# A fused Hyena filter and gated MLP on one core: every other chunk's fraction made by ScalarE and VectorE instead of VectorE and GpSimd

## The chip, the core and the metric

One Trainium2 (trn2) chip, one of its cores. The metric is the device time of one execution in microseconds (us), measured on the chip. The kernel before takes 4258.93 us (median of three runs, 4258.6 to 4264.06; with a fourth run, 4258.99). Engines are named as the profile names them: PE is the matmul engine (PEld its weight loads), DVE is VectorE, ACT is ScalarE, POOL is GpSimd. In the traces each engine starts its instructions in the order of its own queue, and waits there for what another engine has to finish first (an example below: an ACT instruction whose input was ready started 0.71 us later, behind the one in front of it).

## The reference

Shortened:

```python
def _attn_ref(x, v, pos_emb, w1, w2):              # x, v: (4, 12480, 128)
    h_filt = (np.maximum(pos_emb @ w1, 0.0) @ w2) * np.exp(-0.01 * pos)[:, None]
    u = x * v
    y = irfft(rfft(u, 2*S) * rfft(h_filt, 2*S), 2*S)[:, :S, :]      # along the sequence
    return x * y

def _moe_ref(x, w_in, w_out):                      # x: (49920, 128), d_ff = 2048
    h = x @ w_in
    return (h * np.cos(h)) @ w_out
```

A long convolution for each of four batches, then an MLP whose activation is h cos(h). The change touches only the cosine.

## The kernel before

The convolution of a batch is a hand-made two-level Fourier transform, in five stages: u (multiply and fold the inputs; DVE and POOL), f1 (first transform; PE, evicted by ACT and DVE), f2 (second transform and the product with the filter; PE, four DVE products, two POOL sums), i1 and i2 (the inverse). Batch 0 is done first, alone. Then the MLP's *chunks* run, and the convolutions of batches 1 to 3 are woven in between them, one *unit* of convolution work for every 1.2 to 2.3 chunks, by stage (set in the kernel). When they are done, the MLP runs alone to the end. A chunk is 128 of the 2048 hidden columns for a *tile* of 480 tokens: 16 chunks a tile, 104 tiles, 1664 chunks.

cos(h) is made as sin(2 pi f), f being h/(2 pi) + 1/4 minus its nearest integer. So a chunk passes through PE, ACT, DVE, POOL, ACT, DVE and PE again (shortened, `...` and the tiles of cs and gt left out):

```python
def moe_up(pool, n, c):
    ph = ps_h.tile([P, BANK], F32, name="ph")                       # one of 4 PSUM banks
    nc.tensor.matmul(ph[:, 0:TOK], w_in_sb[:, c * P:(c + 1) * P], ats[n][:, :], ...)
    a = pool.tile([P, TOK], F32, name="a", bufs=3)
    nc.scalar.activation(a[:, :], ph[:, 0:TOK], AF.Identity,        # a = h/(2 pi) + 1/4
                         bias=quarter[:, 0:1], scale=INV_TWO_PI)
    k = pool.tile([P, TOK], F32, name="k")
    nc.vector.tensor_scalar(out=k[:, :], in0=a[:, :], scalar1=ROUND,   # k = round(a)
                            scalar2=ROUND, op0=ALU.add, op1=ALU.subtract)
    f = pool.tile([P, TOK], F32, name="f")
    nc.gpsimd.tensor_tensor(f[:, :], a[:, :], k[:, :], op=ALU.subtract)  # f = a - k
    return ph, f

def moe_act(pool, ph, f):
    nc.scalar.activation(cs[:, :], f[:, :], AF.Sin, scale=TWO_PI)
    nc.vector.tensor_tensor(gt[:, :], ph[:, 0:TOK], cs[:, :], op=ALU.mult)
    ...
# main loop, one step a chunk (cut):
for i in range(len(steps) + LAG):
    hidden[i] = moe_up(mpool, n, c)
    gates[i - 1] = moe_act(mpool, *hidden.pop(i - 1))     # one chunk behind
    moe_down(pn, pc, gates.pop(i - LAG))                  # four chunks behind
    ...                                                   # store, next tile's transposes
    while owed > 0.0:
        owed -= next(conv, owed)                          # units of convolution
```

Of the kernel before, what the change touches and what calls it, by code (L numbers as in the profile page):

```python
# [9 lines left out]
F32 = mybir.dt.float32  # L10
U32 = mybir.dt.uint32
AF = mybir.ActivationFunctionType
ALU = mybir.AluOpType
# [3 lines left out]
P = 128  # L17
# [5 lines left out]
TWO_PI = 6.283185  # L23

ROUND = 12582912.0
# [5 lines left out]
def kernel(  # L31
# [38 lines left out]
    nc = tc.nc  # L70
# [38 lines left out]
    cs = const.tile([N2, 3, H], F32, name="cs")  # L109
# [448 lines left out]
    def moe_turn(pool, n):  # L558
        zb = zbs.pop(n)
        pt = ps_h.tile([P, BANK], F32, name="ph")  # L560
        for m in range(TOK // N2):
            transpose(pt[:, m * N2:(m + 1) * N2], zb[:, m, :])
        at = pool.tile([D, TOK], F32, name="at")
        nc.vector.tensor_copy(out=at[:, :], in_=pt[:, 0:TOK])
        ats[n] = at

    def moe_up(pool, n, c):
        ph = ps_h.tile([P, BANK], F32, name="ph")
        nc.tensor.matmul(ph[:, 0:TOK], w_in_sb[:, c * P:(c + 1) * P], ats[n][:, :],  # L569
                         start=True, stop=True)  # L570
        a = pool.tile([P, TOK], F32, name="a", bufs=3)
        nc.scalar.activation(a[:, :], ph[:, 0:TOK], AF.Identity,  # L572
                             bias=quarter[:, 0:1], scale=INV_TWO_PI)
        k = pool.tile([P, TOK], F32, name="k")
        nc.vector.tensor_scalar(out=k[:, :], in0=a[:, :], scalar1=ROUND,  # L575
                                scalar2=ROUND, op0=ALU.add, op1=ALU.subtract)
        f = pool.tile([P, TOK], F32, name="f")
        nc.gpsimd.tensor_tensor(f[:, :], a[:, :], k[:, :], op=ALU.subtract)  # L578
        return ph, f

    def moe_act(pool, ph, f):
        cs = pool.tile([P, TOK], F32, name="cs")
        nc.scalar.activation(cs[:, :], f[:, :], AF.Sin, scale=TWO_PI)  # L583
        gt = pool.tile([P, TOK], F32, name="gt", bufs=4)
        nc.vector.tensor_tensor(gt[:, :], ph[:, 0:TOK], cs[:, :], op=ALU.mult)  # L585
        return gt

    def moe_down(n, c, gt):
        if c == 0:
            accs[n] = ps_acc.tile([P, BANK], F32, name="acc")  # L590
        nc.tensor.matmul(accs[n][:, 0:TOK], w_out_sb[:, c, :], gt[:, :],  # L591
                         start=(c == 0), stop=(c == NFC - 1))

    def moe_evict(pool, n):
        ot = pool.tile([D, TOK], F32, name="ot", bufs=1)
        nc.scalar.copy(out=ot[:, :], in_=accs.pop(n)[:, 0:TOK])
        return ot

    def moe_store(pool, n, ot):
        pt = ps_h.tile([P, BANK], F32, name="ph")  # L600
        for m in range(TOK // N2):
            transpose(pt[0:N2, m * D:(m + 1) * D], ot[:, m * N2:(m + 1) * N2])
        ob = pool.tile([N2, TOK // N2, D], F32, name="ob", bufs=1)
        nc.vector.tensor_copy(out=ob[:, :, :].rearrange("i m d -> i (m d)"),
                              in_=pt[0:N2, :])
        nc.sync.dma_start(
            out[n * TOK:(n + 1) * TOK, :].rearrange("(m p) d -> p m d", p=N2),
            ob[:, :, :])

    with tc.manual_schedule():  # L610
        make_identity(nc, ident)
        with tc.tile_pool(name="psum", bufs=8, space=PSUM) as psum, \
# [67 lines left out]
            wpool = ctx.enter_context(tc.tile_pool(name="weights", bufs=1))  # L680
            w_in_sb = wpool.tile([D, DFF], F32, name="w_in_sb")
            w_out_sb = wpool.tile([P, NFC, D], F32, name="w_out_sb")
            quarter = wpool.tile([P, 1], F32, name="quarter")
            nc.vector.memset(quarter[:, :], 0.25)
            nc.sync.dma_start(w_in_sb[:, :], wind[:, :])
            nc.sync.dma_start(w_out_sb[:, :, :], woutd[:, :, :])
            for stage in (f2_units(bank, f2_product), i1_units(bank)):
# [16 lines left out]
        mpool = ctx.enter_context(tc.tile_pool(name="moe", bufs=2))  # L704
# [18 lines left out]
        def load(n):  # L723
            while ready < n // NT:
                next(conv)
            moe_load(mpool, n)
# [5 lines left out]
        steps = [(n, c) for n in range(NALL) for c in range(NFC)]  # L732
        hidden, gates, ots = {}, {}, {}
        for i in range(len(steps) + LAG):
            if i < len(steps):
                n, c = steps[i]
                if c == 0 and n + 2 < NALL:
                    load(n + 2)
                hidden[i] = moe_up(mpool, n, c)
            if 0 <= i - 1 < len(steps):  # L740
                gates[i - 1] = moe_act(mpool, *hidden.pop(i - 1))
            if i >= LAG:
                pn, pc = steps[i - LAG]
                moe_down(pn, pc, gates.pop(i - LAG))
                if pc == NFC - 1:
                    ots[pn] = moe_evict(mpool, pn)
            if i < len(steps):
                if c == LAG + 1 and n - 1 in ots:
                    moe_store(mpool, n - 1, ots.pop(n - 1))
                if c == NFC // 2 and n + 1 < NALL:  # L750
                    moe_turn(mpool, n + 1)
            owed += share
            while owed > 0.0:
                owed -= next(conv, owed)
# [32 lines left out]
```

## Time and profile before

The stages of the trace, summed over the three woven batches. A stage runs from its first DVE or ACT instruction of its kind to the next stage's; the MLP alone from the last instruction of i2 to the end.

| stretch | before, us | what bounds it |
|---|---|---|
| batch 0's convolution | 638.7 | not touched |
| u | 434.6 | chain over DVE, POOL, ACT; PE has gaps |
| f1 | 546.2 | PE |
| f2 | 788.0 | chain over DVE, POOL, ACT; PE has gaps |
| i1 | 574.7 | PE |
| i2 | 398.3 | PE |
| MLP alone | 882.0 | PE, without a gap |
| span | 4262.5 | |

In a line of the timeline, the first number is the start in us, the second the length, and the bracket at the end says how long the engine had been idle and what ended that.

### The profile page before, as it was taken

Reading aid. Unit: us, or ns where it says so; the run is one execution under the profiler, and the core shown is the slowest. Engines: PE = TensorE matmul, PEld = TensorE weight load, DVE = VectorE, ACT = ScalarE, POOL = GpSimd, SP = SyncE. Lnnn points to the kernel's source line nnn. Section 1 sums busy time; section 2 is a strip of 40 time slices with the busy share of each in tenths; the row PEclk is TensorE's granted clock in tenths of the full one; section 3 lists DMA queues with packets and bytes.
Section 4 is the critical chain, followed back from the end, with each engine's and each line's share of the span. In section 5 each row is a group of like instructions: output and inputs, shape, how many; then the busy total and the mean of one; then the engine's idle time right before and its main releaser. Section 6 shows DMA issues by size and latency. Waiting matters only on the chain.

```text
span 4262.5 us, 49170 instructions
## 1 busy us (share of the span) xinstructions
PE 3916.4 (92%) x13882; PEld 2244.3 (53%) x13882; DVE 3047.8 (72%) x6588; ACT 2415.2 (57%) x4484; POOL 2546.8 (60%) x2311
## 2 busy tenths in 40 slices
PE   5868778999999998998899989988999999999999
PEld 3836673554456653554466634644466644444444
DVE  8657669987778568777776588766675566666666
ACT  1343155775567445655455456644554577777777
POOL 2422347657865457568854476568754577777776
PEclk8557889999999999999999999999999999999999
DMA  3354343112211442012201531022103400000000
GB/s 86 89 167 120 96 136 106 50 52 78 82 51 42 142 142 85 15 50 81 75 12 51 177 112 42 15 73 78 52 15 107 127 19 19 19 19 19 19 19 14
DMA packets 271763, 293.63 MB, mean 69 GB/s; under 512 B 16741, under 2 KB 204101, under 8 KB 271237
## 3 DMA queue, kind: packets, MB, share of 16 engines
q1 hardware_dynamic: 271493, 290.50, 23.6%
q8 instruction: 112, 1.84, 0.2%
q14 instruction: 158, 1.29, 0.1%
HBM read 210.12 MB, written 80.31 MB: 68 GB/s over the span
## 4 chain that ended last, share of the span: by engine, by line
PE 65%; POOL 11%; DVE 10%; ACT 5%; DMA 5%; issue 3%; SPq 0%; DVEq 0%; POOLq 0%; ACTq 0%
PE ph L569 24%; PE acc L591 23%; POOL f L578 6%; POOL slots L369 5%; PE cv L404 4%; PE cv L386 4%; ACT cs L583 3%; PE cv L343 3%; PE ps L343 3%; DVE gt L585 2%; DMA w<-wd 2%; DMA hd<-h 2%; PE ph L116 2%; DVE slots L336 1%; PE ps L386 1%
## 5 line engine op out<-in xcount | busy, mean ns | idle before, releaser
L578 POOL TENSOR_TENSOR f<-a,k 128x480 f32<-128x480 f32 x1664 | 2021.9, 1218 | 1174.9 <-DVE k L575 1174.9
L569 PE MATMUL ph<-at,w_in_sb 128*128 128x480 f32 x3328 | 1647.4, 577 | 102.6 <-DVE gt L585 101.6
L591 PE MATMUL acc<-gt,w_out_sb 128*128 128x480 f32 x3328 | 1618.0, 568 | 0.5 <-DVE gt L585 0.5
L572 ACT ACTIVATE a<-ph,quarter 128x480 f32<-128x480 f32 x1664 | 1094.2, 658 | 750.7 <-PE ph L569 691.8
L585 DVE TENSOR_TENSOR gt<-ph,cs 128x480 f32<-128x480 f32 x1664 | 1091.7, 656 | 476.3 <-ACT cs L583 452.7
L583 ACT ACTIVATE cs<-f 128x480 f32<-128x480 f32 x1664 | 998.4, 600 | 690.6 <-POOL f L578 688.7
L575 DVE TENSOR_SCALAR k<-a 128x480 f32<-128x480 f32 x1664 | 778.8, 468 | 528.3 <-ACT a L572 514.4
L591 PEld LDWEIGHTS acc<-gt,w_out_sb 128*128 128x128 f32 x3328 | 633.8, 190 | 715.5 <-issue 713.5
L569 PEld LDWEIGHTS ph<-at,w_in_sb 128*128 128x128 f32 x3328 | 584.8, 191 | 575.4 <-issue 290.4
L369 POOL TENSOR_TENSOR slots<-slots,t 120x256 f32<-120x256 f32 x384 | 296.6, 795 | 228.2 <-DVE t L368 176.6
L357 PE MATMUL ps<-slots,w 124*120 124x256 f32 x384 | 165.9, 576 | 80.7 <-DVE w L250 45.6
L386 PEld LDWEIGHTS cv<-cs,slots 120*96 120x96 f32 x1536 | 180.5, 168 | 82.0 <-issue 72.1
L357 PE MATMUL cv<-slots,w 124*120 124x256 f32 x576 | 155.3, 390 | 49.7 <-PE acc L591 36.0
L404 PEld LDWEIGHTS cv<-slots,tm 96*104 96x104 f32 x1440 | 173.1, 171 | 46.7 <-issue 36.0
L386 PE MATMUL cv<-cs,slots 120*96 120x120 f32 x1536 | 191.2, 267 | 3.3 <-POOL slots L369 3.3
L404 PE MATMUL cv<-slots,tm 96*104 96x128 f32 x1440 | 178.7, 275 | 11.0 <-DMA tm<-td 7.2
L343 PEld LDWEIGHTS cv<-c,slots 104*124 104x124 f32 x768 | 130.6, 192 | 84.4 <-issue 54.8
L357 PEld LDWEIGHTS ps<-slots,w 124*120 124x120 f32 x384 | 93.0, 268 | 153.0 <-issue 70.5
L357 PEld LDWEIGHTS cv<-slots,w 124*120 124x120 f32 x576 | 98.7, 182 | 134.3 <-PE acc L591 78.0
L343 PE MATMUL cv<-c,slots 104*124 104x192 f32 x768 | 159.5, 330 | 3.2 <-POOL slots L336 2.6
L396 DVE TENSOR_TENSOR slots<-cv,other 96x240 f32<-96x240 f32 x384 | 135.9, 393 | 0.5
L330 POOL TENSOR_TENSOR xt<-xt,vt 104x512 f32<-104x512 f32 x30 | 38.3, 1276 | 137.5 <-DMA vt<-in_v_dram 127.0
(111 smaller groups left out, 2781.8 us busy)
## 6 DMA issues: line engine op xcount, KB each, us to landing
h<-hd SPq DMA_DIRECT2D x192, 240.0 KB
tm<-td SPq DMA_DIRECT2D x90, 312.0 KB
xt<-in_x_dram SPq DMA_DIRECT2D x120, 208.0 KB
vt<-in_v_dram SPq DMA_DIRECT2D x120, 208.0 KB
xs<-in_x_dram SPq DMA_DIRECT2D x120, 208.0 KB
zd<-zs SPq DMA_DIRECT2D x120, 208.0 KB
zb<-zd SPq DMA_DIRECT2D x104, 240.0 KB
out_dram<-ob SPq DMA_DIRECT2D x104, 240.0 KB
```

Of the source, the lines that this page charges most:

```text
L343: nc.tensor.matmul(ps[0:KE, i * 2 * N1:(i + 1) * 2 * N1], u[:, b, 0:KE, i], c1[0:u.shape[0], :, :].rearrange("p r k -> p (r k)"), start=Tr ...
L357: nc.tensor.matmul(ps[0:N2, i * 2 * D:(i + 1) * 2 * D], w[:, i, :], parts[0:KE, :, k1 + i, :, :], start=True, stop=True)
L369: nc.gpsimd.tensor_tensor(y[:, r], y[:, r], t[:, r], op=op)
L386: nc.tensor.matmul(ps[0:N1, (i * 2 + r) * N2:(i * 2 + r + 1) * N2], parts[0:N2, r, :, b, i], cs[:, r:r + 2, :].rearrange("p c a -> p (c a) ...
L404: nc.tensor.matmul(ps[0:R, i * D:(i + 1) * D], t[:, i, r, :], slots[0:N1, :, place, :], start=(r == 0), stop=(r == 1))
L569: nc.tensor.matmul(ph[:, 0:TOK], w_in_sb[:, c * P:(c + 1) * P], ats[n][:, :], start=True, stop=True)
L572: nc.scalar.activation(a[:, :], ph[:, 0:TOK], AF.Identity, bias=quarter[:, 0:1], scale=INV_TWO_PI)
L575: nc.vector.tensor_scalar(out=k[:, :], in0=a[:, :], scalar1=ROUND, scalar2=ROUND, op0=ALU.add, op1=ALU.subtract)
L578: nc.gpsimd.tensor_tensor(f[:, :], a[:, :], k[:, :], op=ALU.subtract)
L583: nc.scalar.activation(cs[:, :], f[:, :], AF.Sin, scale=TWO_PI)
L585: nc.vector.tensor_tensor(gt[:, :], ph[:, 0:TOK], cs[:, :], op=ALU.mult)
L591: nc.tensor.matmul(accs[n][:, 0:TOK], w_out_sb[:, c, :], gt[:, :], start=(c == 0), stop=(c == NFC - 1))
```

## The change

The intent: POOL's subtraction, 1.2 us a chunk, is the slowest step of the chain and shares POOL with the convolution. For odd chunks, the rounded number is made by ACT (a + ROUND) and the fraction by one DVE instruction, which subtracts ROUND and a at once (the sign is undone in the sine's scale).

```diff
--- before.py
+++ after.py
@@ -571,16 +571,25 @@
         a = pool.tile([P, TOK], F32, name="a", bufs=3)
         nc.scalar.activation(a[:, :], ph[:, 0:TOK], AF.Identity,
                              bias=quarter[:, 0:1], scale=INV_TWO_PI)
+        return ph, a
+
+    def moe_fold(pool, a, c):
+
         k = pool.tile([P, TOK], F32, name="k")
-        nc.vector.tensor_scalar(out=k[:, :], in0=a[:, :], scalar1=ROUND,
-                                scalar2=ROUND, op0=ALU.add, op1=ALU.subtract)
         f = pool.tile([P, TOK], F32, name="f")
-        nc.gpsimd.tensor_tensor(f[:, :], a[:, :], k[:, :], op=ALU.subtract)
-        return ph, f
-
-    def moe_act(pool, ph, f):
+        if c % 2 == 0:
+            nc.vector.tensor_scalar(out=k[:, :], in0=a[:, :], scalar1=ROUND,
+                                    scalar2=ROUND, op0=ALU.add, op1=ALU.subtract)
+            nc.gpsimd.tensor_tensor(f[:, :], a[:, :], k[:, :], op=ALU.subtract)
+            return f, TWO_PI
+        nc.scalar.activation(k[:, :], a[:, :], AF.Identity, bias=whole[:, 0:1])
+        nc.vector.scalar_tensor_tensor(out=f[:, :], in0=k[:, :], scalar=ROUND, in1=a[:, :],
+                                       op0=ALU.subtract, op1=ALU.subtract)
+        return f, -TWO_PI
+
+    def moe_act(pool, ph, f, scale):
         cs = pool.tile([P, TOK], F32, name="cs")
-        nc.scalar.activation(cs[:, :], f[:, :], AF.Sin, scale=TWO_PI)
+        nc.scalar.activation(cs[:, :], f[:, :], AF.Sin, scale=scale)
         gt = pool.tile([P, TOK], F32, name="gt", bufs=4)
         nc.vector.tensor_tensor(gt[:, :], ph[:, 0:TOK], cs[:, :], op=ALU.mult)
         return gt
@@ -682,6 +691,8 @@
             w_out_sb = wpool.tile([P, NFC, D], F32, name="w_out_sb")
             quarter = wpool.tile([P, 1], F32, name="quarter")
             nc.vector.memset(quarter[:, :], 0.25)
+            whole = wpool.tile([P, 1], F32, name="whole")
+            nc.vector.memset(whole[:, :], ROUND)
             nc.sync.dma_start(w_in_sb[:, :], wind[:, :])
             nc.sync.dma_start(w_out_sb[:, :, :], woutd[:, :, :])
             for stage in (f2_units(bank, f2_product), i1_units(bank)):
@@ -736,9 +747,13 @@
                 n, c = steps[i]
                 if c == 0 and n + 2 < NALL:
                     load(n + 2)
-                hidden[i] = moe_up(mpool, n, c)
+                ph, a = moe_up(mpool, n, c)
+                if c % 2 == 0:
+                    hidden[i] = (ph,) + moe_fold(mpool, a, c)
             if 0 <= i - 1 < len(steps):
                 gates[i - 1] = moe_act(mpool, *hidden.pop(i - 1))
+            if i < len(steps) and c % 2 == 1:
+                hidden[i] = (ph,) + moe_fold(mpool, a, c)
             if i >= LAG:
                 pn, pc = steps[i - LAG]
                 moe_down(pn, pc, gates.pop(i - LAG))
```

## The prediction

> **What bounds the kernel now.** I read the page first, then the stretches of time in one table, then the chain of waits of single stretches, then the timeline of a quiet stretch.
>
> ```profile
> PE 3916.4 (92%) x13882; PEld 2244.3 (53%) x13882; DVE 3047.8 (72%) x6588; ACT 2415.2 (57%) x4484; POOL 2546.8 (60%) x2311
> ```
>
> PE is busy for 92% of the span, but the average hides stages with different limits. The program is one batch of convolution alone (0 to 634 us, no changed code), three batches of convolution interleaved with the MLP's chunks (634 to about 3385 us), and the MLP alone (to 4262 us). Inside each convolution the stages are u, f1, f2, i1, i2. One stretch of each in the first mixed batch, in that order, and the MLP alone:
>
> ```profile
> core 0: us, PE busy (x) PEld busy (x) DVE busy (x) ACT busy (x) POOL busy (x), PEclk, DMA share, GB/s
> 640.00:780.00 140.00, 117.28 (x274) 46.96 (x273) 127.01 (x191) 74.45 (x129) 106.43 (x92) 0.97 0.33 97
> 790.00:950.00 160.00, 159.71 (x564) 95.39 (x563) 143.61 (x332) 127.92 (x265) 85.38 (x71) 1.00 0.16 45
> 970.00:1210.00 240.00, 218.58 (x638) 111.88 (x637) 174.03 (x394) 122.62 (x211) 195.37 (x191) 1.00 0.29 81
> 1240.00:1400.00 160.00, 160.00 (x763) 100.45 (x762) 129.92 (x307) 112.55 (x246) 81.95 (x68) 1.00 0.14 41
> 1420.00:1540.00 120.00, 120.00 (x627) 82.23 (x626) 64.98 (x118) 52.61 (x90) 51.82 (x43) 1.00 0.58 178
> 3400.00:4250.00 850.00, 850.00 (x2298) 411.91 (x2297) 589.36 (x1085) 650.12 (x1055) 616.03 (x512) 1.00 0.07 18
> ```
>
> PE has no gap in f1, i1, i2 and the MLP alone; it has gaps in u and f2. The chain of waits says the same, for u, f2 and the MLP alone:
>
> ```profile
> by line: POOL f L578 23.3%; issue 14.2%; DVE slots L336 13.4%; ACT cs L583 12.1%; ACT a L572 9.1%; DVE k L575 9.0%; DVE xt L330 5.0%; PE ph L569 4.7%; PE acc L591 3.5%; DVE gt L585 2.8%; DVE at L564 0.9%; ACT L583 0.9%; POOL slots L336 0.9%
> ...
> by line: POOL slots L369 25.8%; POOL f L578 24.3%; DVE gt L585 10.4%; ACT cs L583 10.2%; PE ph L569 7.4%; PE acc L591 5.7%; DVE t L368 5.4%; issue 5.2%; PE cv L357 1.8%; DVE slots L367 1.6%; DVE at L564 1.1%; DVE k L575 0.9%; PE ph L116 0.3
> ...
> by line: PE ph L569 48.5%; PE acc L591 48.4%; PE ph L116 3.1%
> ```
>
> So POOL's subtraction f is on the path only in u (3 x about 143 us) and f2 (3 x about 262 us). That is what the change goes for. In the MLP alone the 512 chunks of 850 us take 1.660 us each, 26.56 us for a tile of 16. But there PE is bound with little in reserve, which the timeline shows (start, length, engine):
>
> ```profile
> 3714.94 0.66 ACT L572 ACTIVATE a<-ph,quarter 128x480 f32<-128x480 f32 x1
> ...
> 3715.70 0.41 DVE L575 TENSOR_SCALAR k<-a 128x480 f32<-128x480 f32 x1 [0.20 <-ACT a L572]
> 3715.82 0.60 ACT L583 ACTIVATE cs<-f 128x480 f32<-128x480 f32 x1 [0.22 <-POOL f L578]
> ...
> 3716.20 1.21 POOL L578 TENSOR_TENSOR f<-a,k 128x480 f32<-128x480 f32 x1 [0.40 <-DVE k L575]
> ...
> 3716.55 0.66 ACT L572 ACTIVATE a<-ph,quarter 128x480 f32<-128x480 f32 x1
> ...
> 3717.43 0.60 ACT L583 ACTIVATE cs<-f 128x480 f32<-128x480 f32 x1 [0.23 <-POOL f L578]
> ...
> 3718.16 0.66 ACT L572 ACTIVATE a<-ph,quarter 128x480 f32<-128x480 f32 x1
> ```
>
> ACT's queue is a(i), cs(i-1), a(i+1), cs(i). The first a above, its k, its f and the cs at 3717.43 belong to one chunk. The a after that cs cannot start before it ends: a loop through ACT, DVE, POOL and ACT that spans two chunks. Its length is 0.66 + 0.10 + 0.41 + 0.09 + 1.21 + 0.02 + 0.60 = 3.09 us (the small terms are the gaps between the lines). PE's two chunks take 3.22 us (3714.94 to 3718.16). The loop has 0.13 us to spare.
>
> **What the Trainium skill says.** "ScalarE: Activation LUTs", section "What ACT_TABLE_LOAD costs", gives 186 ns + 0.833 ns an element with immediate operands, about 93 ns more for each per-partition operand, and 93 ns of overlap back to back. The trace agrees: cs, 602 ns for 480 elements, is 400 + 202; the tk activation (scale by partition, 208 elements) takes 471 = 173 + 298. So the new ACT instruction, whose bias is a per-partition operand, should take 298 + 400 = about 0.70 us, an estimate, not cs's 0.60. "VectorE: DVE Perf Modes", section "The TRN2 errata", gives (N+151)/0.96 ns for an fp32 two-tensor operation: 657 ns at 480; gt takes 658 here. I use 0.66 us for the new DVE f. "SBUF — State Buffer", section "SBUF: two separate sides", says that DVE in a two-port mode or with two SBUF inputs and GpSimd lock each other out. The trace agrees in kind: k averages 676 ns in u, 432 in the MLP alone.
>
> **The change, part by part.** There are 1664 chunks; half, 832, are odd. Each loses a POOL f (1.2 us) and a DVE k (0.41 us or more) and gains an ACT k (0.70) and a DVE f (0.66). Sums: POOL -832 x 1.2 = -1000 us, ACT +832 x 0.70 = +580 us, DVE about +832 x 0.2 = +165 us. As shares of 4262 us that looks harmless: POOL 36%, ACT 70%, DVE 76%. But order counts. I compared the two programs' queues: ACT's is now a(e), cs(o before), a(o), cs(e), k(o); DVE's is k(e), gt(o before), gt(e), f(o). The new ACT k sits behind cs(e), which waits for POOL, and in front of the next pair's a(e).
>
> MLP alone, with time 0 at the end of an ACT k(o): a(e) -0.10 to 0.56 (overlap); DVE f(o) 0.10 to 0.76; DVE k(e) is behind it, 0.78 to 1.19; POOL f(e) 1.27 to 2.48; cs(e) 2.51 to 3.11; k(o) 3.01 to 3.71. The other halves (cs(o) 0.79 to 1.39, a(o), both gt) fit in between. The loop is now 3.71 us a pair, and PE waits for it. Per tile the output copy on ACT (0.54, with overlap 0.44) and DVE's ob copy behind an f(o) (about 0.70) fall into the loop, which they did not before: 8 x 3.71 + 1.14 = 30.8 us a tile against 26.56, or 4.26 more. By the queues, chunks from 1140 on are alone: 524, or 32.75 tiles: **+140 us**.
>
> u: before, the loop of one convolution unit (about 2.1 chunks) is multiply 0.89, sum 0.88, k 0.41, POOL f 1.21, cs 0.60, gt 0.66 with gaps, 4.8 us; measured, 142 us / 30 = 4.7. After, by the queues, 18 of 30 units fall after an even chunk, where only the ACT loop is left (about 3.9), and 12 after an odd one, in front of k(e), where f(o), multiply, sum, k(e), f(e), cs(e), k(o) make 5.2. With two three-chunk steps of 6 and the tiles' share: 16 x 3.9 + 11 x 5.25 + 12 + 4 = 136 us. Three batches: -15 us.
>
> f2: before, a unit takes 262/48 = 5.4 us. After, even to even (19) DVE's queue makes 4.3; odd to odd (15) 5.8, as four products, POOL's slots, f(e), cs(e), k(o), f(o) follow one another; the 13 three-chunk steps about 6.9: 82 + 87 + 90 + 7 for tiles = 266. Three batches: +12 us.
>
> f1 and i1: f1's PE pair is 2 x 2.24 = 4.48 us. The ACT loop with a unit in it (ACT eviction 0.36 net, DVE copies 0.71 in front of k(e)) is 4.4, plus the tile's share: level with PE. In the first batch the tk tables (ACT 0.47, DVE 0.43 a unit) make it 4.8 in f1 and 4.9 in i1 (PE 4.72): +13 and +5. Some loss from unevenness elsewhere: +10. i2's PE pair is 5.5 and hides everything: 0.
>
> Sum: 140 - 15 + 12 + 18 + 10 = +165 us, 4259 + 165 = **4424 us**.
>
> **The rivals.** (1) *POOL was the bound and is relieved.* For it: the u and f2 chains, where POOL has a third to a half of the path and the lock stretches k. If these stages (1215 us) ran 10% faster and the loop did not bind elsewhere: about 4140. Against it: the PE-bound stages (f1, i1, i2, about 1500 us, and the MLP alone, 870 us) cannot gain, and the new ACT instruction is in the same queue. (2) *Nothing moves, PE hides it.* For it: ACT's sum in the MLP alone, 2 x (0.66 + 0.60) + 0.70 - 3 x 0.09 = 2.95 plus the copy, is under PE's 3.32 a pair, so by occupancy it fits: 4250 to 4270. Against it: ACT is idle while it waits for POOL's f(e) in the new loop too, about 0.5 us. (3) *The loop binds harder*: no overlap of activations, or ph buffers that come free late, 3.85 us a pair and f1/i1 10% slower too: about 4520.
>
> **Range and chances.** The MLP alone may lie between 3.6 and 3.85 us a pair (+110 to +180 us), and u with f2 between -70 and +60. Eight in ten: 4355 to 4495. Faster by over 2% needs rival 1 in full: 0.03. Within 2% (up to 4344) needs a loss under 85 us, 80 us less than expected: 0.10. Slower: 0.87.
>
> **What would show it.** In the MLP alone: a period of 3.7 us a pair, the chain of waits passing from PE alone to POOL f, ACT cs, ACT k and DVE k, PE with gaps waiting for gt. The ACT k at 0.70 us, the DVE f at 0.66. u slightly shorter, f2 about level, i2 unchanged. I am wrong if the MLP alone still runs at 1.66 us a chunk with PE at 100%, or if u and f2 shrink by over 100 us in all.

## More of the kernel before

PSUM holds the matmuls' results. The kernel divides eight banks of it: two for acc (the output accumulator), four for ph, two for the convolution's results (cv).

## The result, and the profile after

4371.52 us (median of four runs, 4367.81 to 4379.69) against 4258.99 us: slower by 2.64%, ratio 1.0264, 95% interval 1.0246 to 1.0282. Ratios here are the mean time of one kernel's fast runs over the mean of the other's fast runs of the same rounds, so not quite the ratio of the medians quoted.

The page of the changed kernel: total busy times, and the groups that took the place of the old k and f (busy time and mean ns, then idle time before them).

```profile
PE 3974.8 (91%) x13882; PEld 2224.9 (51%) x13882; DVE 3109.9 (71%) x6589; ACT 2839.6 (65%) x5316; POOL 1503.0 (34%) x1479
...
L583 POOL TENSOR_TENSOR f<-a,k 128x480 f32<-128x480 f32 x832 | 1001.2, 1203 | 2217.3 <-DVE k L581 2196.7
...
L586 DVE SCALAR_TENSOR_TENSOR f<-k,a 128x480 f32<-128x480 f32 x832 | 569.0, 684 | 0.0
L585 ACT ACTIVATE k<-a,whole 128x480 f32<-128x480 f32 x832 | 566.3, 681 | 0.0
```

POOL's load fell by a thousand microseconds, just as intended, and no engine is fuller than PE, which now waits. The busy shares alone do not tell why the kernel is slower. The chain of waits of a stretch of the MLP alone (3480 to 4200 us) does:

```profile
by line: POOL f L583 32.9%; ACT cs L592 16.3%; ACT k L585 16.1%; DVE f L586 11.6%; DVE k L581 11.2%; issue 4.2%; ACT a L572 3.8%; DVE ob L613 2.3%; ACT ot L605 1.5%; DVEq L581 0.1%
```

Before, this line held nothing but PE. Now PE is not in it at all. And the timeline of one pair of chunks there:

```profile
3825.72 0.68 ACT L585 ACTIVATE k<-a,whole 128x480 f32<-128x480 f32 x1
...
3826.31 0.64 ACT L572 ACTIVATE a<-ph,quarter 128x480 f32<-128x480 f32 x1
3826.43 0.66 DVE L586 SCALAR_TENSOR_TENSOR f<-k,a 128x480 f32<-128x480 f32 x1
...
3827.05 0.41 DVE L581 TENSOR_SCALAR k<-a 128x480 f32<-128x480 f32 x1
3827.12 0.60 ACT L592 ACTIVATE cs<-f 128x480 f32<-128x480 f32 x1 [0.18 <-DVE f L586]
...
3827.54 1.20 POOL L583 TENSOR_TENSOR f<-a,k 128x480 f32<-128x480 f32 x1 [2.36 <-DVE k L581]
...
3828.78 0.60 ACT L592 ACTIVATE cs<-f 128x480 f32<-128x480 f32 x1 [0.49 <-POOL f L583]
...
3829.29 0.68 ACT L585 ACTIVATE k<-a,whole 128x480 f32<-128x480 f32 x1
```

Read the starts: from ACT's k to DVE's f 0.71, to DVE's k (of the next even chunk) 0.62, to POOL's f 0.49, to the cs that waits for it 1.24, to the next ACT k 0.51: 3.57 us a pair, while PE needs 3.22. ACT stands idle for 0.18 + 0.49 us of it, and POOL for 2.36, and still nothing can start earlier: the idle engines all wait for one loop.

All ten kernels by stage, from their traces in us (three woven batches summed; the batch 0 part, 636 to 642 us in all of them, is left out). The labels are explained in the next section:

| kernel | u | f1 | f2 | i1 | i2 | MLP alone | median us (runs) |
|---|---|---|---|---|---|---|---|
| before | 434.6 | 546.2 | 788.0 | 574.7 | 398.3 | 882.0 | 4258.99 (4) |
| after | 415.9 | 581.1 | 765.7 | 596.7 | 397.9 | 978.3 | 4371.52 (4) |
| e1_early | 397.6 | 594.6 | 726.2 | 607.6 | 398.8 | 897.4 | 4260.54 (4) |
| e2_twice | 426.2 | 610.1 | 786.6 | 620.7 | 397.4 | 1117.8 | 4600.64 (1) |
| e3_vector | 437.3 | 576.9 | 761.0 | 583.6 | 398.3 | 888.8 | 4286.85 (4) |
| e4_u_f2_only | 414.4 | 546.7 | 764.7 | 576.0 | 398.6 | 882.1 | 4221.22 (4) |
| e5_early_u_f2 | 393.9 | 542.4 | 725.3 | 574.4 | 398.6 | 882.1 | 4159.53 (4) |
| e8_all_u_f2 | 359.9 | 548.7 | 680.8 | 571.5 | 398.0 | 882.1 | 4079.65 (4) |
| e6_after_3banks | 430.1 | 552.5 | 783.7 | 580.1 | 403.9 | 1020.5 | 4410.6 (1) |
| e7_before_3banks | 437.9 | 539.9 | 793.0 | 574.9 | 399.9 | 904.7 | 4293.2 (1) |

The change: u -18.7, f2 -22.3, f1 +34.9, i1 +22.0, i2 -0.4, MLP alone +96.3, and 3.7 before any changed chunk runs, which is scatter (that part varies by 6 us over the ten kernels); 115.4 in all by the spans (4377.9 - 4262.5), up to rounding. The profiled run of either kernel was slower than its other runs; the medians differ by 112.5.

### The profile page after: what moved, and what is told of

Same layout as the page of the kernel before. It is cut to its first block, busy times and chain, and to the rows that moved or that the text cites. A ratio compares the mean times of both kernels' runs of the same rounds, so it can differ in the third digit from the quotient of the medians.

```text
span 4377.9 us, 49056 instructions
## 1 busy us (share of the span) xinstructions
PE 3974.8 (91%) x13882; PEld 2224.9 (51%) x13882; DVE 3109.9 (71%) x6589; ACT 2839.6 (65%) x5316; POOL 1503.0 (34%) x1479
## 4 chain that ended last, share of the span: by engine, by line
PE 38%; DVE 19%; ACT 18%; POOL 13%; issue 7%; DMA 5%; SPq 0%; DVEq 0%; POOLq 0%; ACTq 0%
PE ph L569 12%; POOL f L583 11%; PE acc L600 10%; ACT cs L592 8%; ACT k L585 6%; DVE f L586 5%; PE cv L404 4%; PE cv L386 4%; DVE k L581 3%; PE ps L343 3%; ACT a L572 2%; PE cv L343 2%; POOL slots L369 2%; DVE gt L594 2%; DMA w<-wd 2%
## 5 line engine op out<-in xcount | busy, mean ns | idle before, releaser
L583 POOL TENSOR_TENSOR f<-a,k 128x480 f32<-128x480 f32 x832 | 1001.2, 1203 | 2217.3 <-DVE k L581 2196.7
L586 DVE SCALAR_TENSOR_TENSOR f<-k,a 128x480 f32<-128x480 f32 x832 | 569.0, 684 | 0.0
L585 ACT ACTIVATE k<-a,whole 128x480 f32<-128x480 f32 x832 | 566.3, 681 | 0.0
L581 DVE TENSOR_SCALAR k<-a 128x480 f32<-128x480 f32 x832 | 349.2, 420 | 91.3 <-ACT a L572 87.0
L369 POOL TENSOR_TENSOR slots<-slots,t 120x256 f32<-120x256 f32 x384 | 284.3, 763 | 343.7 <-DVE t L368 295.0
L386 PE MATMUL cv<-cs,slots 120*96 120x120 f32 x1536 | 195.5, 270 | 11.5 <-DVE slots L396 4.9
L343 PE MATMUL cv<-c,slots 104*124 104x192 f32 x768 | 164.0, 336 | 23.4 <-DVE slots L351 14.7
```

The costliest lines, as they stand in the source:

```text
L343: nc.tensor.matmul(ps[0:KE, i * 2 * N1:(i + 1) * 2 * N1], u[:, b, 0:KE, i], c1[0:u.shape[0], :, :].rearrange("p r k -> p (r k)"), start=Tr ...
L386: nc.tensor.matmul(ps[0:N1, (i * 2 + r) * N2:(i * 2 + r + 1) * N2], parts[0:N2, r, :, b, i], cs[:, r:r + 2, :].rearrange("p c a -> p (c a) ...
L585: nc.scalar.activation(k[:, :], a[:, :], AF.Identity, bias=whole[:, 0:1])
L586: nc.vector.scalar_tensor_tensor(out=f[:, :], in0=k[:, :], scalar=ROUND, in1=a[:, :], op0=ALU.subtract, op1=ALU.subtract)
```

## The experiments

The main theory: the place of ACT's k, behind a cs that waits for POOL and in front of the next a, is what costs, not the amount of work. The rival: the amount, that is, ACT (or DVE) simply has too much to do. All eight kernels of the experiments gave correct results. Where rounds were run, the kernel before was timed beside them: 4261.1 us in the first group (e1 to e4), 4261.56 in the second (e5 to e8), medians of 7 runs each.

### e1_early: the same instructions, the odd chunk's k and f in front of the cs

```diff
-                if c % 2 == 0:
-                    hidden[i] = (ph,) + moe_fold(mpool, a, c)
+                hidden[i] = (ph,) + moe_fold(mpool, a, c)
             if 0 <= i - 1 < len(steps):
                 gates[i - 1] = moe_act(mpool, *hidden.pop(i - 1))
-            if i < len(steps) and c % 2 == 1:
-                hidden[i] = (ph,) + moe_fold(mpool, a, c)
```

> The odd chunk's rounding on ScalarE (ACT k) and its DVE f are issued right after that chunk's a, so in front of the even chunk's cs and gt; the same instructions, the same number. Theory (position: the ACT k lies behind a cs that waits for POOL and in front of the next a, so it lengthens the loop a, k, f, cs, k to 3.57 us a pair in the MLP-alone stage): the k falls into ACT's idle time, the loop is about 3.05 us again, under PE's 3.22, and the MLP-alone stage goes from 978 us back to about 882 us, f1 and i1 back to about what they were before the change, u and f2 keep their gain or add to it; total 4140 to 4200 us, faster than before. Rival (amount: half a microsecond more work on ACT and more on DVE for every pair is what costs): the time stays near 4370 us.

4260.54 us, ratio to before 0.9998 (0.9981 to 1.0015): 111 us better than the change, but level with before, not faster. The MLP alone took 897.4 us, and its chain of waits (3480 to 4200 us) is PE's again:

```profile
by line: PE ph L569 48.9%; PE acc L600 47.1%; PE ph L116 3.1%; ACT a L572 0.2%; issue 0.2%; POOL f L583 0.2%; ACT cs L592 0.2%; ACT k L585 0.1%; DVE gt L594 0.1%; ACT ot L605 0.1%; DVE k L581 0.1%; DVEq L581 0.0%
```

So in that stage the place is shown to be the cause: with the same instructions in the same number, 81 of the 96 us are gone. (DVE's f moved forward together with ACT's k, so this run does not tell the one place from the other.) Most pairs are back at 3.22 us; the other 15 us lie in the pairs around a tile's output copy and transposes, 27.1 us a tile against 26.6 before. The gain in u and f2 together more than doubled as well (-37 and -62 us against before). But f1 and i1 did not go back to what they were; they became longer still, 594.6 and 607.6. There the theory fell, and something else had to be found (e6).

### e2_twice: the suspected term doubled

```diff
         nc.scalar.activation(k[:, :], a[:, :], AF.Identity, bias=whole[:, 0:1])
+        again = pool.tile([P, TOK], F32, name="again")
+        nc.scalar.activation(again[:, :], a[:, :], AF.Identity, bias=whole[:, 0:1])
```

> After each ACT k a second activation of the same kind is made, whose result nobody reads. Theory (position in the loop): the MLP-alone pair goes from 3.57 to 3.57 + 0.59 = 4.16 us (0.68 less the overlap), 8 times a tile, 32.75 tiles: +155 us in that stage, 978 to about 1130 us; total above 4600 us. Rival (ACT's total occupancy, now 65%, decides): ACT's sum per pair goes from about 2.95 to 3.54 us, so a pair would be about 3.6 us and the MLP-alone stage near 980 us as in the changed kernel.

One run, so of unknown state: 4600.64 us. A pair in the MLP alone took 4.15 us at the median (4.16 expected), the stage 1117.8 us, 139.5 more than after the change. The rival's 3.6 us a pair is out. So an ACT instruction at this place lengthens the pair by its whole start-to-start time (4.15 - 3.57 = 0.58 us), though ACT has idle time elsewhere in the pair.

### e3_vector: early order, k by DVE, ACT as before the change

```diff
-        nc.scalar.activation(k[:, :], a[:, :], AF.Identity, bias=whole[:, 0:1])
+        nc.vector.tensor_scalar(out=k[:, :], in0=a[:, :], scalar1=ROUND,
+                                scalar2=None, op0=ALU.add)
```

> As the early order, but the odd chunk's rounding is made by DVE (one addition, 0.41 us) instead of ACT; ACT then has no more work than before the change. If position is what counts and ACT's extra work is not: the MLP-alone stage is at about 882 us here too. DVE gets 0.33 to 0.41 us more a pair, so u, where DVE is busy for 91% before the change, should be longer than with the early order by up to 8 us a batch, and f2 by a few us; total 4160 to 4240 us. If the ACT k's amount is what costs, this run gains most of the 112 us and the early order does not.

4286.85 us, ratio 1.0062 (1.0047 to 1.0077), slower than expected. The MLP alone is 888.8 us, 9 better than with ACT's k in the early order: there the amount of ACT work counts for little. u is 437.3, 40 us over e1's, more than the 24 expected, and f2 35 us over it: where DVE is the full engine (here busy for 138 of 140 us in u and 190 of 200 in f2), its 0.4 us cost more than ACT's 0.7. f1 and i1, at 576.9 and 583.6, are again above before, though ACT does nothing new here. So their loss is not ACT's k alone either.

### e4_u_f2_only: the change in its own order, only while the convolution is in u or f2

```diff
+                late = c % 2 == 1 and stage in ("u", "f2")
-                if c % 2 == 0:
+                if not late:
                     hidden[i] = (ph,) + moe_fold(mpool, a, late)
...
-            if i < len(steps) and c % 2 == 1:
+            if i < len(steps) and late:
```

(`stage` is set by the convolution's generator as it enters each stage; `moe_fold` takes the flag instead of the parity.)

> The change in its own order, but only for odd chunks issued while the convolution is in u or f2; elsewhere the kernel of before. By the traces the change gains 19 us in u and 22 us in f2 over three batches and loses 34 in f1, 22 in i1 and i2, 96 in the MLP alone. Theory (effects are local to the stages): about 4259 - 41 = 4218 us, 4205 to 4235. Rival (the gain in u and f2 is only shifted time, given back at the stages' ends): 4250 to 4260 us.

4221.22 us, ratio 0.9908 (0.9893 to 0.9923). Each stage took what one of the two kernels takes there (row of the table), and the sum came out at 4221 for an expected 4218. Effects are local to the stages, the gain is not given back later, and the table may be read stage by stage.

### e6_after_3banks and e7_before_3banks: why f1 and i1 lose

In f1 of the changed kernel the timeline looks like this (columns as before):

```profile
1795.92 0.89 PE L343 MATMUL cv<-c,slots 104*124 104x192 f32 x4 [0.33 <-DVE slots L351]
...
1796.65 0.97 PE L569 MATMUL ph<-at,w_in_sb 128*128 128x480 f32 x2
...
1797.66 0.66 ACT L572 ACTIVATE a<-ph,quarter 128x480 f32<-128x480 f32 x1 [1.14 <-PE ph L569]
1798.22 0.59 ACT L592 ACTIVATE cs<-f 128x480 f32<-128x480 f32 x1
```

PE's convolution matmuls waited for L351, a DVE instruction that empties one of the two cv banks and stands in DVE's queue behind the MLP's f and behind L350, which the trace shows waiting for ACT's eviction L349, and that behind ACT's k (here with a tile's output copy, L605, between them; in a plain pair PE waits likewise, for 0.21 us at 1738.03). The next chunk's matmul stands behind them in PE's queue; ACT sat idle 1.14 us until that matmul was done and its a could start, and the cs behind it, whose f POOL had finished at 1797.51 (its line starts at 1796.30 and lasts 1.21), started only at 1798.22. That is a second loop, through PE and the cv banks, which the prediction did not have. PE waited for L351 for 14.7 us in all, and for L396, its like in i1, for 4.9; in the kernel before, for neither. In e1 the same waits are longer, 26.1 and 14.9 us, which fits its longer f1 and i1, though no run gave e1 a third bank. The test gives the convolution a third bank, taken from the accumulator:

```diff
-        ps_acc = ctx.enter_context(tc.tile_pool(name="ps_acc", bufs=2, space=PSUM))
+        ps_acc = ctx.enter_context(tc.tile_pool(name="ps_acc", bufs=1, space=PSUM))
...
-        ps_c = ctx.enter_context(tc.tile_pool(name="ps_c", bufs=2, space=PSUM))
+        ps_c = ctx.enter_context(tc.tile_pool(name="ps_c", bufs=3, space=PSUM))
```

> The changed kernel with three PSUM banks for the convolution's results instead of two, and one accumulator bank instead of two (there are eight in all). Theory (f1 and i1 lose time in the changed kernel because PE's convolution matmuls wait for one of two banks to be emptied by ACT and DVE, whose queues the change delays, and the next chunk's matmul stands behind them): f1 goes from 581 back to under 560 us, i1 from 597 to under 585, while the MLP alone stays at about 978 or gets a few us longer (one accumulator). Rival (f1 and i1 lose because the ACT loop of 3.57 us grows by the evictions to over PE's period, whatever the banks): f1 and i1 stay at about 581 and 597.

> Control for the run with three banks: the kernel of before with the same banks. f1 and i1 are PE bound there (546 and 575 us), so a third bank should gain nothing, and the single accumulator costs at most half a microsecond for each of 104 tiles: total 4255 to 4310 us, f1 545 to 555, i1 575 to 585.

One run each (4410.6 and 4293.2 us, state unknown, with mean granted clocks of 0.939 and 0.945 against 0.954 to 0.960 in the fast runs of before and after), read by stage only. f1 fell from 581.1 to 552.5 us and i1 from 596.7 to 580.1; in the control f1 went from 546.2 to 539.9 (545 to 555 expected) and i1 from 574.7 to 574.9. So what the change costs in f1 shrank from 34.9 to 12.6 us, and in i1 from 22.0 to 5.2. By these single runs the wait for a bank is about two thirds of the one loss and three quarters of the other. Part of the rest looks like the test's own cost: in the traces PE waited for the single accumulator for 8.6 us in e6's f1 and 3.1 in its i1, and in the control's for none. What then remains is open. PE's busy time (third number, after the stretch and its length) over the same 140 us of f1, before, after the change and with three banks, shows the gap open and close, at a granted clock of 1.00 (third number from the end) in all three:

```profile
1720.00:1860.00 140.00, 139.71 (x488) 82.92 (x487) 103.75 (x237) 93.86 (x182) 75.00 (x63) 1.00 0.05 13
```

```profile
1720.00:1860.00 140.00, 134.17 (x462) 77.30 (x461) 102.64 (x222) 102.93 (x198) 34.92 (x29) 1.00 0.06 15
```

```profile
1720.00:1860.00 140.00, 139.10 (x493) 84.31 (x492) 109.50 (x237) 110.97 (x213) 37.36 (x31) 1.00 0.06 15
```

It is no remedy: the single accumulator cost 23 us in the MLP alone of the kernel before and 42 us of the changed one, more than the few I expected. The traces show PE there waiting for ACT's output copy ot to free the accumulator, for 14.0 us in the control and 85.9 in e6; e6's clock in that stage was also lower (0.96 from 3480 to 4200 us), so how much each costs is not shown.

### e5_early_u_f2 and e8_all_u_f2: what to keep

e5 is e1's order with e4's condition. e8 drops the parity as well:

```diff
-                new = c % 2 == 1 and stage in ("u", "f2")
+                new = stage in ("u", "f2")
```

> The early order (ACT k right after the odd chunk's a), used only for odd chunks issued while the convolution is in u or f2; elsewhere the kernel of before. If stages add up, u takes 398 us and f2 726 us as with the early order everywhere, and f1, i1, i2 and the MLP alone take what they take before the change (546, 575, 398, 882): 4262 - 37 - 62 = about 4163 us, 4150 to 4180, faster than before by over 2%. If the gain of u and f2 is tied to what the other stages do, 4200 or more.

4159.53 us, ratio 0.9761 (0.9745 to 0.9777), as the stages said: faster than both kernels.

> As the run before, but every chunk of u and f2, not every other, gets its fraction from ACT and DVE; POOL is then left to the convolution there. If POOL still were what bounds u and f2, they would shrink further, to under 380 and 700 us, total under 4130. If by now ACT bounds (three activations for each chunk, 2 x (0.57 + 0.59 + 0.59) = 3.5 us a pair at best, and DVE's f in front of gt waits for it), u and f2 take as long or longer than with every other chunk: 4160 to 4230 us.

4079.65 us, ratio 0.9574 (0.956 to 0.9588). I had leaned to ACT as the next bound and was wrong: u shrank from 393.9 to 359.9 and f2 from 725.3 to 680.8. The error was in plain sight: 3.5 us a pair for ACT is less than the pair of e5 in u, 131 us for some 62 chunks, or 4.2 us. In f2 (970 to 1170 us) PE is now nearly full; first e5, then e8:

```profile
970.00:1170.00 200.00, 190.16 (x562) 99.73 (x561) 165.56 (x350) 136.20 (x231) 125.69 (x125) 1.00 0.31 87
```

```profile
970.00:1170.00 200.00, 196.59 (x594) 105.77 (x592) 182.29 (x372) 174.82 (x294) 77.24 (x84) 1.00 0.31 88
```

PE is busy for 196.6 of 200 us, and POOL (seventh number) has fallen to 77. So rival 1 of the prediction had a true core: POOL's f did bound u and f2. Whether by POOL's load or by its 1.2 us in each chunk's chain, where DVE's f takes 0.66, no run separates. In u and f2 together e8 gains 182 us on the kernel before, over four times what the change itself gains there (41).

## Why the prediction was right or wrong

The measured 4371.5 us lies in the range (4355 to 4495), below its centre; slower was given 0.87. The mechanism named for the largest term was the right one. That the total lies in the range is in part luck: had f1 and i1 lost no more than the 28 us forecast, it would be 4343 us, below the range. Every term of the sum can be checked by the table:

- **MLP alone, +140 predicted, +96.3 measured.** Right mechanism, mis-sized: it lies below the stage's own range too (3.6 to 3.85 us a pair, +110 to +180). A pair took 3.57 us, not 3.71. Two gaps were too large: from the start of ACT's k to DVE's f I had 0.70 + 0.10, it was 0.71 (the k lasted 0.68 and f followed 0.03 us behind it); from f to DVE's k 0.68, it was 0.62, as DVE starts an instruction before the line of the one before ends. The tile's share was 1.0 us, not 1.14: two of the eight pairs of a tile take 4.02 and 4.11 us instead of 3.57. That makes 8 x 3.57 + 0.99 = 29.55 us a tile against 26.56, and 32.75 tiles x 2.99 = 98 us. e1 shows that the place of ACT's k and DVE's f is the cause, and e2 that ACT time at k's place counts in full.
- **u, -15 predicted, -18.7 measured.** Right (the prediction's own 142 and 136 us a batch make -18).
- **f2, +12 predicted, -22.3 measured.** Wrong in sign, mostly from one term that the prediction does not print: I gave the four DVE products 0.42 us each, the length of their lines. No run tests this; the kernel before already showed that they start closer together than they last:

```profile
1204.16 0.41 DVE L367 TENSOR_TENSOR slots<-cv,h 120x256 f32<-120x256 f32 x1
1204.49 0.42 DVE L368 TENSOR_TENSOR t<-cv,h 120x256 f32<-120x256 f32 x1
1204.83 0.42 DVE L367 TENSOR_TENSOR slots<-cv,h 120x256 f32<-120x256 f32 x1
```

  The starts are 0.33 us apart. In the changed kernel a unit took on average 4.09 us from even to even (4.3 predicted), 5.58 from odd to odd (5.8) and 6.5 to 7.0 with three chunks (6.9): shapes as predicted, each about 0.2 us shorter, and 48 of them in each of three batches make some 30 us. The old kernel's 5.4 us a unit I took from the trace, so the error did not cancel.
- **f1 and i1, +28 predicted (18 for the tables of the first batch, 10 for unevenness), +57 measured.** The step that failed is "the ACT loop with a unit in it is 4.4, plus the tile's share: level with PE". It left out the loop through PE and the two cv banks; a pair in f1 took 4.97 us at the median, against PE's 4.48, and 4.53 with three banks (e6), which shows that loop as the larger part of the loss. It also is no matter of the first batch: f1 lost 12.6, 11.5 and 10.7 us in the three.
- **i2, 0 predicted, -0.4 measured.** Right.
- **Rival 2** (PE hides it) is out: the chain of the MLP alone has no PE in it. **Rival 3** (3.85 us a pair) is out for the MLP alone too. **Rival 1** was wrong for this change and right for u and f2, where e8 gains more than the 10% it promised.

Against the 115.4 us of the traces the sum of +165 was about 50 us too high: 44 in the MLP alone and 34 in f2, less 29 the other way in f1 and i1; u's 4 and the scatter's 4 cancel.

Smaller slips of the prediction: ACT's k took 0.68 us and not 0.70, as its own figures 186 + 93 + 400 ns would have said; POOL's share of the path in u is a quarter (23.3% + 0.9%), not a third; rival 3's terms (176 us in the MLP alone, 112 in f1 and i1) lead to about 4547 us, not 4520; and ACT's busy time rose by 424 us and DVE's by 62, not by 580 and 165.

## What to carry to other kernels

A step that is moved to an idle engine goes to a place in that engine's queue, and the place decides: behind an instruction that waits and in front of one that others wait for, a 0.68 us instruction on an engine busy for 65% of the span, with the DVE instruction that follows it, cost the MLP alone 96 us; one position earlier they cost that stage 15. Write down the loop that returns to the same engine and compare it with the bound engine's period, with start-to-start times and not lengths. And where stages have different bounds, apply such a change only in the stages where the relieved engine is on the path: that alone turned a loss of 2.6% into a gain of 0.9% (e4), of 2.4% with the early order (e5), and of 4.3% with every chunk (e8).

## What the Trainium skill lacked or had wrong

- "VectorE: DVE Perf Modes", section "The TRN2 errata", gives the length of a two-tensor fp32 operation ((N+151)/0.96 ns, which gt's 656 to 658 ns confirm). Beside the formula it neither says how far two DVE instructions overlap in a profile nor points to where the skill speaks of it. Here products that last 0.42 us start 0.33 us apart, and a k starts 0.04 us before the f in front of it ends. "ScalarE: Activation LUTs", section "What ACT_TABLE_LOAD costs", has such a figure for ACT, 93 ns, and the trace agrees: k starts 0.09 us before cs ends.
- The same page's tables have no row for the scalar_tensor_tensor operation with two SBUF tensors in fp32. It took 684 ns on average over 832 instructions, and 0.66 us in the MLP alone, as the two-tensor formula has it (657).
- "ScalarE: Activation LUTs", section "Rules for kernel authors", says to use VectorE and not ScalarE for additions, by the time an element takes. One addition took 681 ns on ACT and the rounding 420 on DVE, so the lengths agree; but in u and f2, where DVE is the fuller engine, the version with ACT's k (e1) was 40 and 35 us shorter than the one with DVE's (e3), and longer in f1, i1 and the MLP alone. Followed to the letter, the rule picks the slower version in u and f2: it goes by one instruction's time and not by which engine has room in the stage.
- "Perfetto Trace Analysis", section "Identifying the Most-Contended Engine", reads a bottleneck from occupancy (for PE from other measures). In the stretch of the MLP alone (3480 to 4200 us) ACT was busy for 575 of the 720 us after the change, and for 627 with the early order, which is faster there: the fuller engine went with the shorter stage. The bound was a loop through three queues, of which no occupancy tells; the section on the optimization strategy, which follows the gaps and what ends them, is the one that finds it.
